# Retention with a gated MLP on one core: the same steps, planned in another order

## The chip, the cores and the metric

One core of one Trainium2 chip runs the whole kernel. The metric is the device time of one execution in microseconds (us), smaller is better. The time before is 221.45 us, the median of three runs (219.28 to 222.36).

## The reference, cut to what matters

A linear attention with a decaying state (retention) feeds a gated MLP. All arrays are float32: 4 batches, 8 heads of 64, 768 tokens, model width 512.

```
for t in range(S):                                  # retention
    state = gamma * state + outer(k[t], v[t])
    y[t] = scale * q[t] @ state
x = y, heads side by side                           # 4 x 768 x 512
gate = sigmoid(sum over 5 taps of conv_w[k] * x shifted by k - 4)
val = x @ w_val                                     # 512 x 512
out = (gate * val) @ w_out                          # 512 x 512
```

## The kernel before, in words

**Tiling.** The 768 tokens are cut into 6 chunks of 128. A chunk of one batch is a *block*: there are 24, numbered g = 0 to 23, chunk by chunk and batch by batch within a chunk, so blocks 0 to 3 are chunk 0 of the four batches. The decay is folded into factors per token: v is scaled on load (`decay`, L294, GpSimd), and y at the end (`evac`, L446, or `wide_evac`, L399, VectorE). So the state is a plain sum, kept in PSUM (`z_ps`).

**Blocks 0 to 3** use whole chunks of 128 tokens ("wide"): `wide_scores` (L347), two masks on VectorE (L355), `wide_y` (L373), `wide_state` (L393) for the running sum, `wide_evac` into the tile x. **Blocks 4 to 23** work on halves of 64 tokens: one `block` on TensorE is 128 small matmuls in four groups, in this order: L403 with the masked scores u, L324 (state, of this block and the next), L403 with `snap` (a copy of the state that ScalarE takes, L334), and L303, the scores of the *next* block. VectorE then masks those (L312) and evacuates y (L446). So block g+1 waits for a mask on VectorE that waits for block g.

**The MLP** works on a chunk of all four batches (512 columns), n = 0 to 5. x and both weights are each split into a high and a low part (fp32r), and a product is three passes: high by high, low by high, high by low. `val_tile` (L592) is 12 matmuls into one bank, `out_tile` (L620) 12 more; there are 4 of each for each n, 288 matmuls of each kind in all. The gate is 5 taps of a convolution: tap 0 on ScalarE (L567), taps 1 to 4 on VectorE (L569), or one or two of them as a matmul with a diagonal on TensorE (`pe_tap`, L578). After that come a sigmoid (L585), the product with val (L601, VectorE), and its split (L608 ScalarE, L612 GpSimd). x is split by L455 (ScalarE) and L459 (GpSimd).

**Weights** arrive as float64 in eight blocks of 512 KB: n = 0 to 3 are the columns of w_val that `val_tile` m = n needs, n = 4 to 7 the rows of w_out. `convert` makes float32 of them in integer steps on VectorE (`cv_bits` L506 or L512, `cv_top` L518, `cv_exp` L524, `cv_rest` L528, `cv_sum` L535, `cv_flush` L542), each on 128x512; then come `cv_round` (L552, ScalarE) and `cv_low` (L556, GpSimd). A block in `FLUSHED` begins on VectorE (L506) and ends with L542; the others begin with three steps on ScalarE (L493, L497, L501) and L512. `cv_sum` is on GpSimd, or on VectorE for the blocks in `SUM_ON_DVE`.

**What sets the order.** Every step is recorded with a due time; `plan` sorts by due time and simulates all engines with costs written in the file, and each engine's instructions are recorded in the order that results. It also picks, for taps 1 and 2, the engine (VectorE or TensorE) that it thinks is free first. On the chip each engine runs its list in order and waits by semaphores. A table of numbers (L655 to L672) sets the due times. All loads of att and the weights go through one queue, SyncE's (SP). A load there also waits until the load issued eight places before it (counted together with ScalarE's four small loads at the start) has landed, and from block 4 on until the buffer of the block four before is free (`LB = 4`).

## Time and profile before

| | us |
|---|---|
| median of three runs | 221.45 |
| lowest, highest | 219.28, 222.36 |
| the profiled execution, its own time | 218.3 |
| its span in the trace | 216.5 |
| TensorE busy | 200.4 |
| VectorE busy | 138.2 |
| ScalarE busy | 109.1 |
| GpSimd busy | 104.4 |

The span is from the first to the last instruction of the profiled execution; the time has 1.8 us more around it. Matmuls overlap in the pipeline, so that one shown with 400 ns in a row of equal ones starts 233 ns after the one before it (12 in 2.80 us). A float32 matmul shows as two records. The engines are named PE (TensorE), DVE (VectorE), ACT (ScalarE), POOL (GpSimd) and SP (SyncE) in the profile.

### The profile page before, as it was taken

The page shows a single profiled execution, that of the slowest core. Times are in us where ns is not written, and L with a number is a line of the kernel's source. Part 1 is how long each engine was busy: PE and PEld are TensorE (multiplying, and loading weights), DVE is VectorE, ACT ScalarE, POOL GpSimd, SP SyncE. Part 2 cuts the span into 40 slices and gives each one's busy share as a digit, 9 for nine tenths or more (in the row PEclk, how much of TensorE's full clock was granted, in tenths as well). Part 3 has the DMA queues.
Part 4 walks back from the last instruction along what each step waited for, and adds up shares of the span by engine and source line. Part 5 has one row for each costly group of instructions (what it writes and reads, how often), then busy time and mean ns, then how long its engine had stood idle before and what let it go on. Part 6 is the DMA issues. An engine that isn't in the chain of part 4 may idle for free.

```text
span 216.5 us, 7441 instructions
## 1 busy us (share of the span) xinstructions
PE 200.4 (93%) x3293; PEld 159.9 (74%) x3293; DVE 138.2 (64%) x213; ACT 109.1 (50%) x224; POOL 104.4 (48%) x93
## 2 busy tenths in 40 slices
PE   8188778989999979999999999999999999999994
PEld 3077666768778758888887888788878887888883
DVE  1959899988999959943993617982189624811000
ACT  2645386397589367456624276341655356321311
POOL 0264599669995954149515078020835145220400
PEclk9769999999999999999999999999999999999999
DMA  6999999886677576076175011101111111111122
GB/s 220 328 414 418 407 381 334 325 300 233 229 272 272 204 248 232 37 233 242 48 221 224 5 48 51 51 9 42 48 51 48 48 48 51 48 48 48 48 97 100
DMA packets 9396, 36.36 MB, mean 168 GB/s; under 512 B 1170, under 2 KB 1682, under 8 KB 6804
## 3 DMA queue, kind: packets, MB, share of 16 engines
q1 hardware_dynamic: 8928, 35.66, 44.7%
q8 instruction: 26, 0.43, 0.8%
q10 hardware_dynamic: 436, 0.23, 0.4%
q14 instruction: 6, 0.05, 0.1%
HBM read 29.59 MB, written 6.29 MB: 166 GB/s over the span
## 4 chain that ended last, share of the span: by engine, by line
PE 76%; DMA 13%; POOL 4%; DVE 3%; ACT 2%; issue 1%; ACTq 0%; SPq 0%; POOLq 0%
PE mm L620 31%; PE mm L592 29%; DMA att<-in_att_dram 11%; PE sy L403 9%; PE z_ps L324 3%; PE sy L303 3%; DMA small_sb<-in_small_dram 2%; POOL xl L459 1%; DVE acc L569 1%; POOL att L294 1%; ACT xh L455 1%; POOL rest L535 1%; DVE gvl L355 1%; POOL wol L556 1%; PE sy L347 1%
## 5 line engine op out<-in xcount | busy, mean ns | idle before, releaser
L569 DVE SCALAR_TENSOR_TENSOR acc<-x,cw_sb,acc 128x512 f32<-128x512 f32 x95 | 68.9, 751 | 22.8 <-ACT acc L567 21.4
L459 POOL TENSOR_TENSOR xl<-x,xh 128x512 fp32r<-128x512 f32 x24 | 30.7, 1296 | 33.6 <-PE mm L592 32.1
L612 POOL TENSOR_TENSOR gvl<-gate,gvh 128x512 fp32r<-128x512 f32 x24 | 30.8, 1295 | 30.6 <-ACT gvh L608 21.0
L620 PE MATMUL mm<-wol,gvh 128*128 128x512 f32 (+1 forms) x100 | 38.9, 389 | 1.1 <-POOL wol L556 1.1
L620 PE MATMUL mm<-woh,gvh 128*128 128x512 f32 (+1 forms) x100 | 39.0, 390 | 0.7 <-ACT woh L552 0.7
L620 PE MATMUL mm<-woh,gvl 128*128 128x512 f32 (+1 forms) x100 | 38.9, 389 | 0.0
L294 POOL TENSOR_TENSOR att<-att,small_sb 128x512 f32<-128x512 f32 x24 | 25.1, 1047 | 24.6 <-DMA att<-in_att_dram 23.6
L630 ACT COPY o_sb<-mm 128x512 f32<-128x512 f32 (+1 forms) x25 | 14.2, 569 | 38.8 <-PE mm L620 37.4
L601 DVE TENSOR_TENSOR gate<-mm,gate 128x512 f32<-128x512 f32 x24 | 16.5, 686 | 26.9 <-PE mm L592 26.6
L592 PE MATMUL mm<-xh,wvh 128*128 128x512 f32 x96 | 27.2, 402 | 1.6 <-ACT xh L455 1.6
L592 PE MATMUL mm<-xl,wvh 128*128 128x512 f32 x96 | 27.6, 400 | 0.0
L592 PE MATMUL mm<-xh,wvl 128*128 128x512 f32 x96 | 27.4, 398 | 0.0
L608 ACT CAST gvh<-gate 128x512 fp32r<-128x512 f32 x24 | 14.9, 620 | 18.0 <-DVE gate L601 12.1
L620 PEld LDWEIGHTS mm<-wol,gvh 128*128 128x128 f32 x100 | 18.8, 188 | 5.5 <-POOL wol L556 1.4
L620 PEld LDWEIGHTS mm<-woh,gvh 128*128 128x128 f32 x100 | 18.8, 188 | 5.0 <-ACT woh L552 0.9
L592 PEld LDWEIGHTS mm<-xh,wvh 128*128 128x128 f32 x96 | 17.6, 188 | 5.8 <-ACT xh L455 1.7
L620 PEld LDWEIGHTS mm<-woh,gvl 128*128 128x128 f32 x100 | 18.8, 188 | 4.1
L592 PEld LDWEIGHTS mm<-xh,wvl 128*128 128x128 f32 x96 | 17.9, 187 | 4.4
L592 PEld LDWEIGHTS mm<-xl,wvh 128*128 128x128 f32 x96 | 17.7, 188 | 4.5 <-POOL xl L459 0.4
L585 ACT ACTIVATE gate<-acc 128x512 f32<-128x512 f32 x24 | 14.3, 597 | 8.9 <-POOL gvl L612 6.1
L334 ACT COPY snap<-z_ps 128x256 f32<-128x256 f32 x40 | 13.4, 374 | 9.4 <-PE z_ps L324 6.6
L403 PEld LDWEIGHTS sy<-u,att 64*64 64x64 f32 x640 | 11.2, 134 | 8.6 <-issue 2.9
(59 smaller groups left out, 263.1 us busy)
## 6 DMA issues: line engine op xcount, KB each, us to landing
att<-in_att_dram SPq DMA_DIRECT2D x20, 1024.0 KB, 6.2
out_dram<-o_sb SPq DMA_DIRECT2D x23, 256.0 KB, 2.0
wst<-in_w_dram SPq DMA_DIRECT2D x8, 512.0 KB, 7.2
att<-in_att_dram SPq DMA_DIRECT2D x3, 768.0 KB, 8.0
att<-in_att_dram SPq DMA_DIRECT2D x5, 256.0 KB, 7.1
att<-in_att_dram SPq DMA_DIRECT2D x1, 512.0 KB, 6.2
out_dram<-o_sb SPq DMA_DIRECT2D x2, 128.0 KB, 1.7
small_sb<-in_small_dram ACTq DMA_DIRECT2D x1, 132.0 KB, 4.3
```

What stands on the lines that cost most here:

```text
L294: nc.gpsimd.tensor_tensor(v, v, vd_sb[:, c, :].unsqueeze(2).broadcast_to([P, 8, HALF]), op=ALU.mult)
L334: nc.scalar.copy(sn, z_ps[:, :, b])
L403: return nc.tensor.matmul(sy[cols, h, off:off + HALF], lhsT=lhsT, rhs=rhs, start=start, stop=True, skip_group_check=True,)
L459: nc.gpsimd.tensor_tensor(xl[n, ct], xs[n][:, ct, :, HALO:], xh[n, ct].bitcast(F32), op=ALU.subtract)
L569: nc.vector.scalar_tensor_tensor(acc, x[:, :, k:k + P], cw_sb[:, m, k:k + 1], acc, op0=ALU.mult, op1=ALU.add,)
L585: nc.scalar.activation(gate[n, m], accs.pop((n, m)), AF.Sigmoid)
L592: nc.tensor.matmul(vps[n, m], lhsT=w[:, m, ct * P:(ct + 1) * P], rhs=xx[n, ct].rearrange("p b t -> p (b t)"), start=(i == 0), stop=(i == 3 ...
L601: nc.vector.tensor_tensor(gv, vps.pop((n, m)), gv, op=ALU.mult)
L608: nc.scalar.copy(gvs[n, m][0], gate[n, m])
L612: nc.gpsimd.tensor_tensor(gvl, gate.pop((n, m)), gvh.bitcast(F32), op=ALU.subtract)
L620: nc.tensor.matmul(ops[n, b, cs.start][:, 0:cs.stop - cs.start], lhsT=gg[:, b * P:(b + 1) * P], rhs=w[:, ct, cs], start=(i == 0), stop=(i ...
L630: nc.scalar.copy(o_sb[:, 0:step], ops.pop((n, b, cs.start))[:, 0:step])
```

## The change

Only the table of numbers changes; every step is still issued once, with the same arithmetic but for three choices: which weight blocks are in `FLUSHED` (five instead of four) and in `SUM_ON_DVE` (two instead of one), and, through the plan, which taps run on TensorE.

```
-    FIRST_LOADS = ((1, 0), (1, 3), (2, 0), (1, 2), (0, 0), (2, 1), (0, 1), (0, 2), (2, 3), (2, 2), (1, 1), (0, 3))
+    FIRST_LOADS = ((1, 0), (0, 0), (1, 1), (1, 2), (2, 1), (0, 1), (1, 3), (2, 0), (0, 2), (0, 3), (2, 2), (2, 3))
...
-    EARLY = 8
+    EARLY = 4
...
-    FLUSHED = (0, 1, 3, 5)
-    SUM_ON_DVE = (3,)
-    BLOCK_AT = (13.32, 26.32, 26.83, 30.27, 39.38, 40.32, 41.28, 42.46, 50.05, 61.09, 68.2, 73.5, 87.54, 92.41, 106.28, 109.98, 121.37, 143.92, 150.84, 184.37)
-    MLP_AT = 39.032
-    MLP_STEP = 4.954
+    FLUSHED = (1, 3, 4, 6, 7)
+    SUM_ON_DVE = (2, 6)
+    BLOCK_AT = (19.76, 27.31, 33.34, 34.76, 39.48, 49.38, 53.2, 56.21, 59.31, 73.82, 79.97, 91.86, 116.18, 119.19, 135.61, 150.42, 153.74, 173.95, 179.78, 208.52)
+    MLP_AT = 28.529
+    MLP_STEP = 8.666
...
-    W_AT = (1.65, 22.94, 24.49, 3.36, 48.39, 41.58, 43.9, 62.46)
+    W_AT = (2.01, 28.62, 23.78, 15.85, 35.37, 56.67, 42.47, 61.42)
```

**SyncE's queue, its first loads before.** 128x1024 of wst is a weight block (512 KB); att_129, att_155, att_178 and att_198 are blocks 0 to 3 and att_279 is block 4; 128x1024 of att is q and k of block 0, 128x1536 is q, k by dimension and v (768 KB), and 128x512 is v of block 0 or the k by token (256 KB). wst_119, wst_124, wst_136 and wst_229 are weight blocks 0, 3, 2 and 1.

```order
L469 DMA wst_119<-in_w64_dram 128x1024
L469 DMA wst_124<-in_w64_dram 128x1024
L282 DMA att_129<-in_att_dram 128x512
L469 DMA wst_136<-in_w64_dram 128x1024
L282 DMA att_129<-in_att_dram 128x1024
L282 DMA att_129<-in_att_dram 128x512
L282 DMA att_155<-in_att_dram 128x512
L282 DMA att_155<-in_att_dram 128x1536
L282 DMA att_178<-in_att_dram 128x1536
L282 DMA att_198<-in_att_dram 128x512
L282 DMA att_178<-in_att_dram 128x512
L469 DMA wst_229<-in_w64_dram 128x1024
```

The thirteenth is q, k and v of block 3. The same queue now, where att_124, att_159, att_207 and att_220 are blocks 0 to 3, and wst_135, wst_140 and wst_178 are weight blocks 1, 2 and 3:

```order
L469 DMA wst_119<-in_w64_dram 128x1024
L282 DMA att_124<-in_att_dram 128x1024
L282 DMA att_124<-in_att_dram 128x512
L469 DMA wst_135<-in_w64_dram 128x1024
L469 DMA wst_140<-in_w64_dram 128x1024
L282 DMA att_159<-in_att_dram 128x512
L282 DMA att_159<-in_att_dram 128x1536
L469 DMA wst_178<-in_w64_dram 128x1024
L282 DMA att_124<-in_att_dram 128x512
L282 DMA att_207<-in_att_dram 128x1536
L282 DMA att_220<-in_att_dram 128x1536
L282 DMA att_207<-in_att_dram 128x512
```

The thirteenth is now the k by token of block 3. The thirteen carry the same bytes. Block 0 has moved from the fifth to the second place, and its k by token from the third to the ninth. Further down, weight block 4 now stands between blocks 6 and 7, where before the next weight blocks stood behind block 7; and on GpSimd's list the sum (L535) of weight block 1 now stands behind the scaling (L294) of block 7, and before stood ahead of that of block 5.

**TensorE, blocks 0 to 3 before,** from the first wide scores to the start of block 4 (L347 scores, L393 state, L373 y):

```order
L347 MATMUL sy<-att 128x128 x8
L393 MATMUL z_ps<-att 64x64 x8
L347 MATMUL sy<-att 128x128 x8
L373 MATMUL mm<-gvl,att 64x128 x8
L393 MATMUL z_ps<-att 64x64 x8
L347 MATMUL sy<-att 128x128 x8
L373 MATMUL mm<-gvl,att 64x128 x8
L393 MATMUL z_ps<-att 64x64 x8
L373 MATMUL mm<-gvl,att 64x128 x8
L347 MATMUL sy<-att 128x128 x8
L393 MATMUL z_ps<-att 64x64 x8
L373 MATMUL mm<-gvl,att 64x128 x8
```

And now, in the same place:

```order
L347 MATMUL sy<-att 128x128 x8
L373 MATMUL mm<-gvl,att 64x128 x8
L347 MATMUL sy<-att 128x128 x8
L393 MATMUL z_ps<-att 64x64 x16
L347 MATMUL sy<-att 128x128 x8
L373 MATMUL mm<-gvl,att 64x128 x8
L393 MATMUL z_ps<-att 64x64 x16
L347 MATMUL sy<-att 128x128 x8
L373 MATMUL mm<-gvl,att 64x128 x16
```

The states of blocks 2 and 3 (the second L393 x16) now stand ahead of the scores of block 3; before, each state stood behind the scores of its block.

**VectorE, from the evacuation of block 3 on, before.** u is the mask of blocks 4 and 5; wst and acc with L518, L524 and L528 are conversions; L569 is the convolution of val tile 0:

```order
L399 TENSOR_TENSOR x<-mm,base 128x4x128
L312 TENSOR_TENSOR u<-sy,small_sb 128x512
L518 SCALAR_TENSOR_TENSOR top<-wst,acc 128x512
L542 SCALAR_TENSOR_TENSOR rest<-acc,rest 128x512
L524 TENSOR_SCALAR acc<-top 128x512
L528 SCALAR_TENSOR_TENSOR rest<-wst,acc 128x512
L569 SCALAR_TENSOR_TENSOR acc<-x,cw_sb,acc 128x512 x3
L446 TENSOR_TENSOR x<-sy,dec 128x4x128
L312 TENSOR_TENSOR u<-sy,small_sb 128x512
```

And now:

```order
L399 TENSOR_TENSOR x<-mm,base 128x4x128
L518 SCALAR_TENSOR_TENSOR top<-wst,acc 128x512
L524 TENSOR_SCALAR acc<-top 128x512
L312 TENSOR_TENSOR u<-sy,small_sb 128x512
L528 SCALAR_TENSOR_TENSOR acc<-wst,acc 128x512
L535 TENSOR_TENSOR rest<-acc,top 128x512
L569 SCALAR_TENSOR_TENSOR acc<-x,cw_sb,acc 128x512
L506 TENSOR_SCALAR acc<-wst 128x512
L569 SCALAR_TENSOR_TENSOR acc<-x,cw_sb,acc 128x512
L518 SCALAR_TENSOR_TENSOR top<-wst,acc 128x512
L569 SCALAR_TENSOR_TENSOR acc<-x,cw_sb,acc 128x512
L446 TENSOR_TENSOR x<-sy,dec 128x4x128
```

Between the evacuation of block 3 and the mask of block 5 there stood nine instructions, and now eleven (the mask of block 5 is the next row); a conversion stands between the taps. From the mask of block 4 to that of block 13, VectorE's list holds the kinds in this table, which counts from just behind the evacuation of block 3 to just ahead of the mask of block 13:

| VectorE | before | now |
|---|---|---|
| steps of conversions | 18 | 28 |
| taps L569 | 19 | 17 |
| masks L312 and evacuations L446 | 18 | 18 |
| products L601 | 4 | 5 |
| in all | 59 | 68 |

How far TensorE's list has come in the MLP when a block begins (matmuls of val, of out, and taps on TensorE issued ahead of it):

| ahead of block | val, out, taps before | val, out, taps now |
|---|---|---|
| 5 | 7, 0, 0 | 8, 0, 1 |
| 8 | 30, 0, 0 | 36, 0, 1 |
| 9 | 36, 0, 0 | 48, 0, 1 |
| 11 | 48, 0, 1 | 59, 0, 2 |
| 13 | 60, 7, 1 | 63, 9, 3 |
| 14 | 67, 9, 1 | 70, 12, 3 |
| 15 | 72, 14, 1 | 72, 24, 3 |
| 19 | 117, 60, 1 | 111, 60, 3 |
| 23 | 204, 152, 1 | 156, 96, 3 |

The list has three taps on TensorE now and had one before; VectorE's taps go from 95 to 93.

14 lines of the change are left out of this document (7 added, 7 removed).

## The prediction

> **What bounds the kernel now.** I read the page first, then the table by windows, the chain of waits, the timelines of TensorE and VectorE, and the DMA issues.
>
> ```profile
> DMA  6999999886677576076175011101111111111122
> ...
> 20.00:80.00 60.00, 52.95 (x1608) 42.06 (x1605) 53.62 (x85) 39.69 (x89) 48.95 (x42) 1.00 0.81 296
> 80.00:200.00 120.00, 119.91 (x1475) 97.16 (x1475) 71.95 (x106) 56.13 (x106) 45.50 (x37) 1.00 0.24 87
> ```
>
> The first row is the busy tenths of the DMA engines in 40 slices of 5.4 us. In the windows the columns are length, then the busy time of PE, PEld, DVE, ACT and POOL, then clock, DMA share and GB/s. From 80 us on TensorE never stops (119.91 of 120 us), so from there the end is a sum of matmuls whose number no order changes. Only what happens before 80 us counts: up to 20 us the DMA engines are full (digits of 9), and from 20 to 80 us VectorE is busy 53.62 of 60 us, as much as TensorE (52.95).
>
> ```profile
> 5.01 6.19 DMA att<-in_att_dram
> ...
> 11.21 10.72 DMA att<-in_att_dram
> ...
> 21.98 1.19 PE sy L347 x16
> ...
> 23.19 1.29 DVE gvl L355 x2
> ```
>
> This is the chain of waits. Block 0 lands at 11.20, block 3 at 21.93; its scores and masks follow. x of chunk 0 is whole when VectorE has evacuated block 3:
>
> ```profile
> 26.18 0.68 DVE L399 TENSOR_TENSOR x<-mm,base 128x512 f32<-128x512 f32 x1
> 26.78 0.68 DVE L312 TENSOR_TENSOR u<-sy,small_sb 128x512 f32<-128x512 f32 x1
> ...
> 68.00 0.68 DVE L312 TENSOR_TENSOR u<-sy,small_sb 128x512 f32<-128x512 f32 x1
> ...
> 26.78:68.00 41.22, 37.58 (x1217) 30.14 (x1218) 38.19 (x61) 30.19 (x69) 37.15 (x32) 1.00 0.80 289
> ```
>
> That is at 26.78, and the second row is the mask of block 4, the third that of block 13. Between them VectorE is busy 38.19 of 41.22 us. Behind the last mask, TensorE goes on:
>
> ```profile
> 69.05 0.69 PE L403 MATMUL sy<-u,att 64*64 64x64 f32 x32
> ...
> 76.21 0.50 PE L620 MATMUL mm<-woh,gvh 128*128 128x512 f32 x1 [0.74 <-ACT woh L552]
> 77.79 0.50 PE L620 MATMUL mm<-wol,gvh 128*128 128x512 f32 x1 [1.08 <-POOL wol L556]
> ...
> 78.36 0.39 PE L592 MATMUL mm<-xh,wvl 128*128 128x512 f32 x1
> ```
>
> Block 13 starts at 69.05. Two last waits, 0.74 and 1.08 us, are for the last weight block. I take 78.36 as the mark: there blocks 4 to 14, 67 matmuls of val, 12 of out and one tap are done, and no wait follows that counts.
>
> **The first stage: block 0 ahead of three weight blocks.** The head of SyncE's queue keeps its sizes (512, 512, 256, 512 KB), so I take its landings over, with other contents.
>
> ```profile
> 0.74 0.85 SPq L469 DMA_DIRECT2D wst<-in_w_dram  x2
> 1.63 0.42 SPq L282 DMA_DIRECT2D att<-in_att_dram  x1
> 2.10 0.43 SPq L469 DMA_DIRECT2D wst<-in_w_dram  x1
> ...
> wst<-in_w_dram SPq DMA_DIRECT2D x1, 512.0 KB, 5.0
> att<-in_att_dram SPq DMA_DIRECT2D x1, 256.0 KB, 6.6
> ...
> wst<-in_w_dram SPq DMA_DIRECT2D x1, 512.0 KB, 7.8
> ```
>
> The second load (issued at about 1.2) lands after 5.0 us, at 6.2; the third at 8.2; the fourth at 9.9. So q and k of block 0 land at about 6.2 instead of 11.20, and its scores start 5 us earlier. I cost this gain at nothing: before x of chunk 0 is whole, block 3 must be in, and the thirteen first loads carry the same bytes as before, over DMA engines that are full. Their last landed at 21.93. Now the last is a piece of 256 KB, and I put it at 21.3, a little earlier, because its predecessor was three times as long. But the order of TensorE puts the state of block 3, which needs that piece, ahead of the scores of block 3.
>
> ```profile
> 14.71 1.16 PE L347 MATMUL sy<-att 64*128 64x128 f32 x16 [0.34 <-DVE gvl L355]
> 15.80 1.09 PE L373 MATMUL mm<-gvl,att 128*64 128x128 f32 x16
> 16.73 0.63 PE L393 MATMUL z_ps<-att 128*64 128x64 f32 x16
> ```
>
> From 21.3: the state 0.63, the scores 1.16, the two masks 1.29, y 1.09, the evacuation 0.68, in all 4.85, give 26.15; with 0.25 for the hand-overs, 26.4. Before it was 26.78. So five microseconds earlier at block 0 become 0.4 at the stage's end. What hides them is the transfer of the rest, with ends at 24.2 (below) and 27.1 (the last piece at 22.0).
>
> **The second stage: VectorE between the evacuation of block 3 and the mask of block 13.** The list holds 59 instructions there before, and 68 now: ten more steps of conversions (the beginnings on VectorE, two sums taken from GpSimd, the later blocks converted sooner), one product more and two taps fewer. Their mean busy time is 38.19 / 61 = 0.626 us, where 61 are the records that the window touches. 68 of them are 42.6 us, if VectorE never waits. With all that VectorE waited before, one instruction is 41.2 / 59 = 0.699 us, and 68 are 47.5. Which end? Before, part of the waiting was of one tap for the next on the same accumulator:
>
> ```profile
> 30.36 2.34 DVE L569 SCALAR_TENSOR_TENSOR acc<-x,cw_sb,acc 128x512 f32<-128x512 f32 x3 [0.39 <-ACT acc L567]
> 33.81 0.74 DVE L569 SCALAR_TENSOR_TENSOR acc<-x,cw_sb,acc 128x512 f32<-128x512 f32 x1
> 34.46 0.68 DVE L506 TENSOR_SCALAR acc<-wst 128x512 int32<-128x512 int32 x1
> ```
>
> Three taps in a row take 2.34 us, 0.78 each; a tap with other work behind it lets that start after 0.65. The new order sets a conversion between the taps. The waits for TensorE and ScalarE stay: behind each mask another mask stands that needs TensorE's block in between, and tap 0 and the sigmoids are queued behind ScalarE's snaps. I take 1.8 us of waiting out of the 3.0 before: 42.6 + 1.8 = 44.4. The mask of block 13 then starts at 26.4 + 44.4 = 70.8 and TensorE's block 13 at about 71.45, 2.4 us later than before.
>
> TensorE has more done by then: 63 + 9 matmuls and three taps against 60 + 7 and one.
>
> ```profile
> 59.38 0.86 PE acc L578 x2
> ...
> 196.58 2.80 PE mm L592 x12
> ```
>
> A matmul is 2.80 / 12 = 0.233 us, a tap on TensorE 0.86 us (one matmul is two records). The two taps more are 1.72 us that the kernel did not have on this engine; they save VectorE 1.3 us, which the count above contains. They are on the path, since TensorE is full afterwards.
>
> **To the mark.** From 71.45: block 13, 2.03 (below); then 7 matmuls of val and 3 of out, 2.33, which makes 75.8; the waits for the last weight block, 0.74 and 1.08 before, should be gone, for its L528 now stands three places ahead of the mask of block 13 on VectorE, and stood five behind it. The mask of block 14 is seven VectorE instructions behind that of block 13: 70.8 + 0.6 + 7 x 0.626 = 75.8, no later. Block 14 ends at 77.85.
>
> ```profile
> 33.94 0.69 PE L403 MATMUL sy<-u,att 64*64 64x64 f32 x32 [0.92 <-DVE u L312]
> 35.97 0.50 PE L592 MATMUL mm<-xh,wvl 128*128 128x512 f32 x1
> ```
>
> These rows are the start of block 5 and the first matmul behind it: a block without a stall is 35.97 - 33.94 = 2.03 us. At 77.85 are done blocks 4 to 14, 70 of val, 12 of out, and all three taps: against the mark three matmuls more, 0.70 us. So TensorE is 78.36 - 77.85 + 0.70 = 1.2 us ahead of before.
>
> **After the mark.** What is left is 9 blocks and the rest of the matmuls on both sides. The blocks come earlier relative to the MLP (block 23 after 252 matmuls instead of 356). The cover for that is VectorE's slack of 48 us in 120 (71.95 busy), and a load of 1 MB per block at 2.6 us (0.4 MB/us) against blocks at least 4 us apart. Were that cover gone, each late mask would cost its wait in full, as the 0.92 us ahead of block 5 did. I take nothing.
>
> **The sum.** The profiled execution took 218.3 us, with a span of 216.5; 218.3 - 1.2 = 217.1. The median of the runs is 3.2 higher than that execution, so for the median 221.45 - 1.2 = 220.2. The three runs lie from 1% below to 0.4% above their median, so what this measurement can tell from no change is about 2%, 4.4 us.
>
> **The rivals.**
>
> *Slower: TensorE's clock falls in the starved first stage.*
>
> ```profile
> 7.60:14.40 6.80, 3.13 (x32) 2.72 (x32) 4.79 (x8) 3.85 (x10) 3.54 (x3) 0.50 1.03 414
> 14.40:22.00 7.60, 6.24 (x114) 5.69 (x114) 6.86 (x15) 4.66 (x15) 3.56 (x4) 1.00 1.02 408
> ...
> 11.24 2.08 PE L347 MATMUL sy<-att 64*128 64x128 f32 x16 [4.78 <-DMA att<-in_att_dram]
> 13.25 1.12 PE L393 MATMUL z_ps<-att 128*64 128x64 f32 x16
> ```
>
> Before, the granted clock was 0.50 from 7.6 to 14.4 us, around TensorE's wait for block 0, and the scores took 2.08 us there instead of 1.16, the state 1.12 instead of 0.63. Now the same work of blocks 0 to 3 is drawn out from 6.5 to 26 us, with gaps from 7.6 to 10 and up to 14, so half clock may last longer. If it is 0.50 up to the evacuation of block 3, state, scores and y of block 3 take 2.9 us longer; if it stays for two further spans of 3.4 us while TensorE waits for VectorE's masks, up to 3.4 more. 220.2 + 6.3 = 226.5. It decides where TensorE is busy less than about 3.13 of 6.80 us from 18 us on; against it stands that half-speed work itself fills that time. [...] Chance 0.09 for the whole, and 0.08 for the 2.9 alone (223.1).
>
> *Faster: the last loads of blocks 2 and 3 land by their latency, not by the bytes ahead of them.*
>
> ```profile
> att<-in_att_dram SPq DMA_DIRECT2D x3, 768.0 KB, 8.0
> att<-in_att_dram SPq DMA_DIRECT2D x5, 256.0 KB, 7.1
> eye_sb<-in_eye_dram ACTq DMA_DIRECT2D x1, 64.0 KB, 8.0
> ...
> 2.12 0.45 ACTq L285 DMA_DIRECT2D eye_sb<-in_eye_dram  x1
> ```
>
> q, k and v of block 3 go out once eye_sb has landed (2.12 + 8.0 = 10.1), so could land at 18.1, and its last piece, issued when the load eight places ahead lands (5.01 + 6.19 = 11.2, a load of the same size in the same place before), at 18.3. Then the masks of block 2 on VectorE are what is late, and x of chunk 0 is whole at 24.2, 2.2 us sooner; with the lower end of VectorE's waits (0.5 us instead of 1.8) the gain is 1.2 + 2.2 + 1.3 = 4.7: 216.7. Against it: 10.72 us for 768 KB in the chain. [...] Chance 0.16.
>
> *No gain: GpSimd stands before a load while a weight waits behind it.*
>
> ```profile
> POOL att L294 <- DMA att<-in_att_dram: 23.6, 12, 6.5
> ```
>
> GpSimd takes its list in order, and waited 23.6 us for loads. Now weight block 1's sum stands behind the scaling of block 7, whose load is behind that of weight block 4 in SyncE's queue. If such a load took 10.72 us instead of the 7 of the other loads, val tile 1 and all that follows start about 3 us later: 223.2. Chance 0.13.
>
> **How the numbers follow.** The forecast has 0.54, and its own range is from 218.5 (VectorE waits 0.5 us, with 0.4 for the scatter of the runs) to 223.3 (all the waits of before, 47.5 us). Faster by over 2% (below 217.0): the faster rival's 0.16 and 0.01 of scatter, 0.17. Slower (over 225.9): the clock's 0.09 and 0.03 for the last two mechanisms together, 0.12. The rest is 0.71. The range from 216.6 to 224.0 leaves out the full clock case, the pairs, and the edge of the faster rival.
>
> **What would show it.** Right: first wide scores at 6.5 to 7 us; the last evacuation L399 between 25.5 and 27.2; the mask of block 13 at 69.5 to 73; TensorE over 99% busy from 80 us on. Wrong: a clock of 0.50 after 20 us; an L399 before 25; waits of TensorE for masks behind 80 us; or GpSimd waits ahead of L535 or L556 that hold up the second val tile.

## The result, and the profile after

The changed kernel took 221.31 us, the median of 21 runs (218.94 to 223.53); the kernel before, beside it, 220.6, the median of 21 (219.1 to 223.29). The ratio is 1.0067, with a 95% interval from 1.0040 to 1.0094: not 1.2 us faster, as forecast, but by this ratio about 0.7% slower. That ratio leaves out runs more than 1.5% above the fastest of their kernel; the runs of these two kernels spread over 2% and more without a gap, so with the experiments the medians of all runs stand too, with 95% intervals from resampling the runs. By those, with all runs of this study together, the changed kernel is at 221.15 (37 runs), before at 220.58 (128 runs): 0.6 us slower (0.2 to 1.1).

The profiled execution of the changed kernel took 218.94 us (span 217.1), that of before 218.3 (216.5). Of the changed kernel, the windows (length; busy PE, PEld, DVE, ACT, POOL; clock; DMA share; GB/s), and then VectorE's and TensorE's timelines:

```profile
20.00:80.00 60.00, 53.71 (x1626) 42.56 (x1627) 56.51 (x90) 36.99 (x82) 48.25 (x42) 1.00 0.79 292
80.00:200.00 120.00, 119.91 (x1475) 96.92 (x1474) 71.49 (x105) 54.96 (x104) 45.40 (x37) 1.00 0.25 90
```

```profile
24.87 0.69 DVE L399 TENSOR_TENSOR x<-mm,base 128x512 f32<-128x512 f32 x1
...
70.03 0.68 DVE L312 TENSOR_TENSOR u<-sy,small_sb 128x512 f32<-128x512 f32 x1
```

```profile
7.46 1.16 PE L347 MATMUL sy<-att 64*128 64x128 f32 x16
...
31.56 0.28 PE L403 MATMUL sy<-att,snap 64*64 64x64 f32 x4 [1.95 <-issue]
...
44.87 0.27 PE L324 MATMUL z_ps<-att 64*64 64x64 f32 x2 [0.37 <-issue]
...
71.06 0.69 PE L403 MATMUL sy<-u,att 64*64 64x64 f32 x32
...
75.61 0.69 PE L403 MATMUL sy<-u,att 64*64 64x64 f32 x32
76.12 0.65 PE L324 MATMUL z_ps<-att 64*64 64x64 f32 x32
76.59 0.65 PE L403 MATMUL sy<-att,snap 64*64 64x64 f32 x32
77.06 0.65 PE L303 MATMUL sy<-att 64*64 64x64 f32 x31
79.35 0.21 PE L303 MATMUL sy<-att 64*64 64x64 f32 x1 [1.65 <-issue]
```

From 80 to 200 us TensorE is as full as before (119.91 of 120). x of chunk 0 is whole at 25.56 (before 26.86), the mask of block 13 is at 70.03, block 13 at 71.06, block 14 at 75.61, and the two waits for the last weight block are gone: all within 0.9 us of the forecast or better. But one matmul record short of the end of block 14, TensorE stands for 1.65 us. The releaser is "issue": the profile shows no semaphore and no data that it waited for. The chain of waits has this stall on it, and the page's table of queues one for instructions:

```profile
29.61 1.95 issue
...
77.70 1.65 issue
```

```profile
q8 instruction: 26, 0.43, 0.8%
```

26 transfers of 16 KB for 3297 matmul records and as many weight loads: about one transfer per 128 matmul records. Before, from 20 us on, TensorE's row has these "issue" stalls:

```profile
30.63 0.28 PE L403 MATMUL sy<-att,snap 64*64 64x64 f32 x3 [0.35 <-issue]
...
44.17 0.62 PE L403 MATMUL sy<-att,snap 64*64 64x64 f32 x26 [0.50 <-issue]
...
48.88 0.27 PE L324 MATMUL z_ps<-att 64*64 64x64 f32 x2 [0.41 <-issue]
```

They are 1.26 us in sum; now there are 1.95, 0.37 and 1.65, in sum 3.97. The waits for data that TensorE's rows show from 26 to 100 us fell by about as much, from 4.3 us to 1.4: in these two profiles the new order did remove waits, and the stalls took the gain back.

### The profile page after: what moved, and what is told of

It is laid out like the page before. It is cut to its first block, busy times and chain, and to the rows that moved or that the text cites. A ratio compares the mean times of both kernels' runs of the same rounds, so it can differ in the third digit from the quotient of the medians.

```text
span 217.1 us, 7461 instructions
## 1 busy us (share of the span) xinstructions
PE 203.7 (94%) x3297; PEld 161.1 (74%) x3297; DVE 138.1 (64%) x213; ACT 107.0 (49%) x222; POOL 103.1 (47%) x92
## 3 DMA queue, kind: packets, MB, share of 16 engines
q1 hardware_dynamic: 8928, 35.66, 44.4%
## 4 chain that ended last, share of the span: by engine, by line
PE 78%; DVE 7%; DMA 5%; issue 3%; ACT 3%; POOL 1%; SPq 0%; ACTq 0%; DVEq 0%; POOLq 0%
PE mm L620 31%; PE mm L592 29%; PE sy L403 8%; DMA att<-in_att_dram 3%; PE sy L303 3%; PE z_ps L324 3%; DMA small_sb<-in_small_dram 2%; PE sy L347 1%; PE z_ps L393 1%; DVE u L312 1%; DVE acc L569 1%; DVE x L446 1%; ACT diag L575 1%; DVE x L399 1%; DVE rest L528 1%
## 5 line engine op out<-in xcount | busy, mean ns | idle before, releaser
L569 DVE SCALAR_TENSOR_TENSOR acc<-x,cw_sb,acc 128x512 f32<-128x512 f32 x93 | 68.0, 752 | 21.3 <-ACT acc L567 20.2
L620 PE MATMUL mm<-woh,gvh 128*128 128x512 f32 (+1 forms) x100 | 39.5, 395 | 0.0
L294 POOL TENSOR_TENSOR att<-att,small_sb 128x512 f32<-128x512 f32 x24 | 25.1, 1047 | 27.1 <-DMA att<-in_att_dram 27.0
L592 PE MATMUL mm<-xh,wvh 128*128 128x512 f32 x96 | 28.4, 410 | 0.8 <-DVE gate L601 0.7
L601 DVE TENSOR_TENSOR gate<-mm,gate 128x512 f32<-128x512 f32 x24 | 16.5, 687 | 19.1 <-PE mm L592 19.1
L592 PE MATMUL mm<-xl,wvh 128*128 128x512 f32 x96 | 26.9, 398 | 0.0
L592 PE MATMUL mm<-xh,wvl 128*128 128x512 f32 x96 | 26.7, 396 | 0.0
L592 PEld LDWEIGHTS mm<-xl,wvh 128*128 128x128 f32 x96 | 17.8, 187 | 6.2 <-issue 1.9
L620 PEld LDWEIGHTS mm<-woh,gvh 128*128 128x128 f32 x100 | 18.8, 188 | 4.7 <-ACT woh L552 0.4
L592 PEld LDWEIGHTS mm<-xh,wvh 128*128 128x128 f32 x96 | 17.6, 188 | 5.9 <-DVE gate L601 1.5
L620 PEld LDWEIGHTS mm<-wol,gvh 128*128 128x128 f32 x100 | 18.8, 188 | 4.1 <-POOL wol L556 0.2
L620 PEld LDWEIGHTS mm<-woh,gvl 128*128 128x128 f32 x100 | 18.8, 188 | 4.1
L592 PEld LDWEIGHTS mm<-xh,wvl 128*128 128x128 f32 x96 | 17.9, 188 | 4.2
L446 DVE TENSOR_TENSOR x<-sy,dec 128x512 f32<-128x512 f32 x20 | 13.7, 686 | 8.6 <-PE sy L303 8.3
```

The lines of the kernel that those rows point to most:

```text
L294: nc.gpsimd.tensor_tensor(v, v, vd_sb[:, c, :].unsqueeze(2).broadcast_to([P, 8, HALF]), op=ALU.mult)
L446: nc.vector.tensor_tensor(xs[c][:, :, b, HALO:].rearrange("p (h j) t -> p h j t", h=2), sy[:, :, 256:512].rearrange("p h (j t) -> p h j t" ...
L569: nc.vector.scalar_tensor_tensor(acc, x[:, :, k:k + P], cw_sb[:, m, k:k + 1], acc, op0=ALU.mult, op1=ALU.add,)
L592: nc.tensor.matmul(vps[n, m], lhsT=w[:, m, ct * P:(ct + 1) * P], rhs=xx[n, ct].rearrange("p b t -> p (b t)"), start=(i == 0), stop=(i == 3 ...
L601: nc.vector.tensor_tensor(gv, vps.pop((n, m)), gv, op=ALU.mult)
L620: nc.tensor.matmul(ops[n, b, cs.start][:, 0:cs.stop - cs.start], lhsT=gg[:, b * P:(b + 1) * P], rhs=w[:, ct, cs], start=(i == 0), stop=(i ...
```

## The experiments

**The theories.** T1, assumed from the count above (26 transfers for 3297 records): TensorE's instructions come in pages of 128 matmul records, the fetch of a page starts when the one before it begins, and where a page is used up faster than the fetch takes, TensorE stalls. By the traces a block is 128 matmul records (64 float32 matmuls, not 128) in 2.03 us, so by T1 a page that falls on a block is used up fastest; the new order changed which work stands where the pages turn. T2: half clock in the starved first stage costs the time, and the stalls are chance. T3: the stall in block 14 is a wait for data that the trace doesn't show.

**Shifting the page turns (three runs).** Tiny matmuls on TensorE shift every later record by their number. In the changed kernel they stand where it waits anyway. The edit, with n = 4 and 20 in the changed kernel and 20 in before:

```
+        def pad(n):
...
+            for _ in range(n):
+                nc.tensor.matmul(
+                    ys[0][:, 0, 0:1], lhsT=warm.broadcast_to([P, P]), rhs=warm,
+                    start=True, stop=True, skip_group_check=True,
+                )
...
         for step in plan(steps):
+            if step.fn is wide_y and step.args == (0,):
+                pad(n)
             step.fn(*step.args)
```

> The changed kernel with 4 tiny bf16 matmuls (128x1) more on TensorE while it waits for the masks of block 0; they write a bank that is overwritten, so no work is left out and nothing after them changes but the count of TensorE's instructions, by 4 matmul records. T1 (a TensorE instruction page of 128 matmul records is fetched as the one before it begins and comes too late where a page is used up faster than the fetch): the page that ended at 77.7 us now ends 4 records sooner in the block, so the stall of 1.65 us inside block 14 shrinks to about 0.8, the one of 1.95 at 29.6 stays near there, and the time falls by 0.5 to 0.9 us against the changed kernel (ratio to before 1.003 instead of 1.007). T2 (the slower clock in the starved first stage costs the time, and the stalls are chance): stalls and time are as in the changed kernel, ratio 1.007. T3 (the stall in block 14 is a wait for data that the trace does not show): the stall stays 1.65 us at the same matmul.

> The same with 20 tiny matmuls (128x1). T1: the page ends move by 20 records, so the stall leaves block 14; the slowest fetch now falls into a block at 60 to 67 us with about 1.0 us of stall, and that at 29.6 us moves 20 records ahead. Time 0.3 to 1.0 us below the changed kernel, ratio to before 1.002 to 1.005. T2: stalls at other places, but the time stays as in the changed kernel, ratio 1.007, with the same spread of the granted clock. T3: 1.65 us of stall stay in block 14 at the same matmul.

> The kernel before with 20 tiny bf16 matmuls (128x1) more on TensorE at the same place (ahead of y of block 0, where it waits). T1: the page ends, which lay well for this order, now lie badly: a new stall of about 1.5 us inside a block at 66 to 69 us, of which the waits of 0.74 and 1.08 us for the last weight block at 75 to 78 us take up part, so the time is 0 to 1.0 us above before, ratio 1.000 to 1.005. T2 and T3: no new stall, ratio 1.000.

Measured: 4 in the changed kernel, median 1.0 us above before (-0.1 to 2.1; ratio 1.0054, 1.0011 to 1.0097); 20 in it, 2.2 above (1.2 to 3.5; 1.0119, 1.0062 to 1.0175); 20 in before, 4.6 above (1.9 to 5.8; 1.0128, 1.0044 to 1.0213). The largest stalls in TensorE's timeline, first with 4, then with 20, then of before with 20:

```profile
80.76 0.34 PE L303 MATMUL sy<-att 64*64 64x64 f32 x5 [1.85 <-issue]
```

```profile
67.17 0.59 PE L578 MATMUL acc<-x,diag 128*128 128x512 f32 x1 [0.67 <-issue]
70.77 0.33 PE L303 MATMUL sy<-att 64*64 64x64 f32 x2 [0.75 <-issue]
76.03 0.45 PE L303 MATMUL sy<-att 64*64 64x64 f32 x11 [0.69 <-issue]
81.67 0.57 PE L303 MATMUL sy<-att 64*64 64x64 f32 x21 [0.91 <-issue]
```

```profile
47.32 0.60 PE L324 MATMUL z_ps<-att 64*64 64x64 f32 x12 [2.23 <-issue]
...
76.97 0.21 PE L303 MATMUL sy<-att 64*64 64x64 f32 x1 [1.73 <-issue]
```

The number of matmul records ahead of each such stall, counted in the trace:

```
before           347  730   858
before, 20 more  347  730  1113  1623
changed          347  729  1750
changed, 4 more  347  729  1750
changed, 20 more 729 1367  1495  1622  1750  1878
```

All lie on 347 plus a multiple of 128, or up to 5 records short of it. The shortfall is TensorE's other instructions: with the weight loads and the semaphore instructions of the trace counted in, the places are 705 (347 + 347 + 11), 1473 (730 + 731 + 12) and 3521 (1750 + 1751 + 20), which is 705 plus 3 and plus 11 times 256. (Another "issue" wait, 0.84 us ahead of record 31 of the changed kernel, is on no such place: it ends 0.10 us after the first mask of block 0 and looks like a wait for that.) With 4 more the stall stayed at record 1750, and so now stands five matmul records from the end of the block instead of one: it goes with the count, not with the instruction. T3 is out. T1's place is right and its sizes are wrong: the stall with 4 more was to shrink to 0.8 and is 1.85, and 20 more made four stalls of 0.7 to 0.9 out of one, with a sum (3.86) that is hardly less. In before, 20 matmuls that compute nothing cost 4.6 us, more than the whole change; its stalls rose from 1.26 to 4.84 us in sum, and two of them have half clock behind them (0.50 from 46.90 to 50.30 and from 77.60 to 81.00). But this price is not of the shift alone, for in before TensorE does not wait at this place:

```profile
16.72 0.69 PE L931 MATMUL mm<-const-float32-0.0 128*128 128x1 bf16 x20
17.34 1.97 PE L373 MATMUL mm<-gvl,att 128*64 128x128 f32 x16
```

The 20 take 0.62 us there themselves, and x of chunk 0 is whole at 28.44, against 26.86 and 27.62 in the two profiles of before.

One reason why the sizes are off shows in the DMA share around block 14, of the changed kernel and then with 4 more:

```profile
75.00:76.00 1.00, 1.00 (x27) 0.59 (x30) 1.00 (x3) 0.59 (x1) 1.00 (x2) 1.00 0.98 418
76.00:77.00 1.00, 1.00 (x83) 1.00 (x76) 0.96 (x3) 0.81 (x2) 0.44 (x1) 1.00 1.01 418
77.00:78.00 1.00, 0.70 (x48) 0.56 (x40) 1.00 (x2) 1.00 (x3) 0.20 (x1) 1.00 0.64 234
```

```profile
77.00:78.00 1.00, 1.00 (x78) 1.00 (x77) 0.96 (x3) 0.61 (x2) 0.67 (x1) 1.00 1.03 426
78.00:79.00 1.00, 0.91 (x59) 0.78 (x52) 1.00 (x2) 1.00 (x3) 0.00 (x0) 1.00 0.84 318
```

In both, the load of a block fills the DMA engines while block 14 runs. The fetch starts at 76.89 in the one and at 78.48 in the other, 1.28 and 1.65 us after the start of block 14, each time as the load ends; it takes 0.9 us, and TensorE goes on 1.35 to 1.55 us after that. The end of the fetch is what ends these stalls: all 61 "issue" stalls over 0.15 us in the 19 traces from 20 to 90 us end 1.2 to 1.6 us after a fetch has landed. What differs is how late the fetch begins and how long the page before lasts by itself (us; runs that stand further down are among them):

```
                     at record  fetch begins  it     page without  stall  from its end
                                after turn    takes  the stall            to TensorE
changed                1750     1.28          0.90   2.24          1.65   1.56
changed, third         1750     1.61          1.00   2.24          1.93   1.42
changed                 347     3.66          1.03   3.98          1.95   1.23
before, 20 more         730     4.08          0.99   4.24          2.23   1.40
changed, 97 more        730     3.91          0.97   3.71          2.64   1.47
```

In block 14 the page is short; at records 347 and 730 it is the fetch that begins late. What makes it begin late is not shown: at record 1750 of the changed kernel the fetch begins as a load ends (DMA share 1.01, then 0.64, above), but at its record 347 the engines are still full when the fetch begins, at 29.30 (1.07 from 29 to 30 us, 1.00 from 30 to 31), so the end of a load is not always what lets it through. Nor does the fetch start when the page before it begins, as T1 had it: in this table it is 1.28 to 4.08 us later.

The places, then, go by 256 of TensorE's instructions, weight loads among them, as counted above. And a turn can cost much in kernels of this case without added matmuls too: up to 2.33 us, at record 347 with five matmuls moved into block 14 (below).

**Second and third profiles, no edit.**

> The changed kernel once more, unaltered, for a second profile. T1, with what the last runs added (the fetch of TensorE's second page is 16 KB on one DMA engine; where it is served while the last loads of the first stage are on that engine, the last of them lands 1.4 us later; and a TensorE stall that leaves a clock window of 3.41 us less than about two thirds busy makes the next window half speed): either the fetch is served at about 19 us and x of chunk 0 is whole at 26.2 to 26.4 us, or at 21 us and it is whole at 24.9 as in the first profile; a stall of 1.6 to 1.9 us at matmul record 1750 in both; a half-clock window behind it in part of the runs. Ratio to before 1.004 to 1.010. Rival (the first profile is typical, and the pads themselves made x of chunk 0 late): 24.9 again.

> The changed kernel unaltered, on the same chip, for the comparison: median of all runs 0.4 to 1.1 us above before. In its profile by T1: a stall of 1.6 us or more at the page turn in block 14, 4 us or more at page turns in sum, x of chunk 0 whole at 25.5 to 25.9 us (or 1.4 later, where the fetch of the second page is served at about 19 us).

> The kernel before once more, unaltered, for a second profile. T1: the same stalls at matmul records 347, 730 and 858, each under 0.8 us and 1.3 us in sum within 0.6; x of chunk 0 whole at 25.4 to 26.8 us, by whether the fetch at about 19.5 us is served ahead of the last load's slowest part; no half clock after 20 us. Rival: stalls at other records or of other sizes, as chance would have them.

Measured: the changed kernel 0.8 us above before (-0.3 to 1.4; ratio 1.0066, 1.0023 to 1.0109) and 0.9 above (-0.5 to 3.0; 1.0151, 1.0101 to 1.0202). Its stall in block 14 came each time, 1.65, 1.94 and 1.93 us; the sum of "issue" stalls was 3.97, 4.45 and 3.61 (4 or more had been expected of the third). Before has 1.26, and now 0.77 and 0.96 = 1.73, but at records 474 and 1879, not at 347, 730 and 858 as expected: the turns are fixed, which of them hurts is not. Its x of chunk 0 was whole at 27.62, later than expected. TensorE of the changed kernel, third profile, its timeline and the windows behind the stall:

```profile
80.89 0.21 PE L303 MATMUL sy<-att 64*64 64x64 f32 x1 [1.93 <-issue]
```

```profile
81.62:85.03 3.41, 3.41 (x10) 2.64 (x9) 3.38 (x6) 1.22 (x2) 1.78 (x2) 0.50 0.32 127
85.03:88.00 2.97, 2.97 (x133) 2.51 (x131) 1.60 (x3) 1.86 (x5) 0.50 (x1) 1.00 0.13 49
```

Behind the stall the clock is 0.50 from 81.62 to 85.03, for 3.41 us, and 1.00 after that. From the start of block 13 to the end of the last matmul it is 142.9 and 143.2 us in the first two profiles, and 144.7 in this one (144.8 with 4 more, where the clock is 0.50 from 81.86 to 85.26): that window costs 1.6 us on top of the stall. Counted in windows of 3.41 us from 16.65, where the half clock of the first profile ended, the same stall was spread over two of them there (0.38 and 1.27 us), and the clock stayed at 1.00. So the profiled execution was a lucky one. In the second profile it is the stall at record 347 that has such a window behind it, from 32.8 to 36.2 us.

The second thing that varies is the last load of the first stage, the 256 KB piece of block 3. Its landing is told in sixteen parts, as many as the profile counts DMA engines; the last two, and when the first 16 KB on the queue for instructions went out:

```
                     15th    16th   fetch, its us
changed             20.44   20.49   21.25  1.06
changed, second     20.48   20.66   21.45  1.10
changed, third      20.51   21.99   19.25  1.12
changed, 4 more     20.53   21.98   19.15  1.12
```

In all traces it goes with that first fetch: where it begins at 19.57 us or sooner (10 traces), the last part lands 1.0 to 1.5 us behind the fifteenth, where it begins at 19.81 or later (9), 0.3 or less. With 97 more it begins at 13.75, and from the load that lands at 16.12 on, every load up to 21.86 has its last part about 1.2 us late: it looks as if one of the engines, which are full (share 1.01 from 9.82 to 16.64 and 1.06 from there to 20 us in the first profile), stays behind by the fetch. x of chunk 0 is whole at 27.07 in the third profile, at 25.56 and 25.74 in the others.

**The clock in the first stage (four runs).** In the changed kernel, eighteen bf16 matmuls of 128x512 and two tiny ones in the waits for block 0 and block 1; in before, four f32 matmuls of zeros in its wait for block 0, or 8 tiny ones with the same page turns. The edit in the changed kernel (`fills` calls `fill`, which stands in it, L378, and is not used there), and that in before:

```
+            if step.fn is wide_y and step.args == (0,):
+                pad(2)
+                fills(0, 10)
+            if step.fn is wide_scores and step.args == (1,):
+                fills(1, 8)
             step.fn(*step.args)
```

```
+        def pad(n):
...
+                nc.tensor.matmul(
+                    ys[0].rearrange("p a t -> p (a t)"), lhsT=zero.broadcast_to([P, P]), rhs=zero.broadcast_to([P, 512]),
...
         for step in plan(steps):
+            if step.fn is wide_scores and step.args == (0,):
+                pad(4)
             step.fn(*step.args)
```

> The changed kernel with 20 bf16 matmuls more on TensorE, as many as in the run with 20 tiny ones (so the page ends lie alike), but 18 of them 128x512: ten at the wait for the masks of block 0 (8.6 to 10.6 us), eight at the wait for block 1 (12.6 to 13.5). They keep TensorE busy where it starved and write banks that are overwritten. T1: the same time as with the 20 tiny ones, within 0.5 us, since x of chunk 0 is late by the loads. T2: the clock stays at 1.00 from 10 to 17 us, its mean rises to about 0.995, the scores and the state there take 1.16 and 0.63 us instead of 2.08 and 1.2, x of chunk 0 is whole 0 to 0.5 us sooner, the spread of the runs shrinks, and the median is 1 us or more below that with the 20 tiny ones.

> The kernel before with four f32 matmuls of zeros (128x512, 8 matmul records) in TensorE's wait for block 0 (7 to 11 us); they write a bank that is overwritten. T2 for before (the half clock after that wait lasts until 14.4 us in the first profile and until 18.8 in the second, and makes x of chunk 0 whole at 26.9 or at 27.6): the clock stays at 1.00 through the first stage, its mean in the runs rises from about 0.969 to 0.985 or more, x of chunk 0 is whole at 26.9 or sooner in every run, and the time is 0.5 to 1.5 us below the same kernel with 8 tiny ones. If the clock in the first stage costs before nothing, as it cost the changed kernel nothing: the same time as with 8 tiny ones, within 0.5 us.

> The kernel before with 8 tiny bf16 matmuls (128x1) at the same place: the page turns of the run with four f32 matmuls, without their hold on the clock. T1: by the durations of before's pages without their stalls this alignment has no page under 3.6 us, as little as now, so ratio 0.997 to 1.003. T2: mean clock 0.961 to 0.977 as in before.

> The kernel before with four f32 matmuls of zeros in TensorE's wait for block 0, once more, beside the changed kernel and before on one chip. T2 for before: median of all runs 0.8 to 1.6 us below that of before, and 1.5 to 2.3 below the changed kernel, mean clock 0.99 to 1.00 in all runs. If the last run was luck of the chip: within 0.5 us of before.

Measured in the changed kernel: 1.5 us above before (0.0 to 2.1; ratio 1.0087, 1.0044 to 1.0131). The clock is full, and the last evacuation starts 0.1 us sooner than with 20 tiny ones (26.23):

```profile
9.82:16.64 6.82, 6.17 (x77) 3.85 (x76) 4.30 (x11) 2.21 (x7) 3.72 (x4) 1.00 1.02 396
```

```profile
26.11 0.69 DVE L399 TENSOR_TENSOR x<-mm,base 128x512 f32<-128x512 f32 x1
```

The median is 0.7 below that with 20 tiny ones (-2.4 to -0.2), between the two expectations, and 6 and 12 runs can't settle that. At a mean clock of 0.99 to 1.00 its runs still spread from 219.7 to 223.4, so T2 is not what spreads them.

In before it is otherwise. The window behind its wait for block 0, in its first profile, its second, and with the four matmuls:

```profile
14.40:18.80 4.40, 4.09 (x72) 3.78 (x74) 3.66 (x10) 1.49 (x6) 3.56 (x4) 1.00 1.03 405
```

```profile
14.40:18.80 4.40, 4.34 (x44) 4.11 (x46) 2.38 (x6) 1.19 (x5) 3.15 (x3) 0.50 1.02 403
```

```profile
14.40:18.80 4.40, 4.40 (x84) 4.09 (x83) 3.40 (x9) 1.24 (x5) 3.15 (x4) 1.00 1.03 405
```

In the second profile the half clock lasts to 18.80 instead of 14.40, TensorE starts 44 matmul records there instead of 72, and x of chunk 0 is whole at 27.62 though the last load landed at 20.56; with the matmuls it is 26.83. Of 107 runs of before, 67 have a mean clock of 0.969 or less, where half clock for 3.41 us is 0.008 (half of 3.41 in a span of 217); its first profile had 0.983. The 67 have a median of 221.05 us, the other 40 of 219.44. With the four matmuls: 1.3 us below before (-2.5 to 0.0; ratio 0.9993, 0.9947 to 1.0039), and again 1.9 below (-3.1 to 0.3; 1.0022, 0.9971 to 1.0073); with 8 tiny ones 0.7 below (-2.4 to 1.4; 0.9993, 0.9941 to 1.0045). The ratios and the medians of all runs agree: the four matmuls don't beat before's good runs, they make the others rare. Their 24 runs have a median of 219.04, against 220.57 of the 39 runs of before beside them (-2.5 to -0.3), and 2.1 us below the changed kernel (1.6 to 3.0). It is the best version found here. The 8 tiny matmuls and the four large ones have the same page turns, but not the same stalls: 3.15 us in sum in the profile of the one, 0.76 and 1.55 in those of the other, and the first of these spans 215.8 us against 218.1. So the sum changes from profile to profile by as much as between the two orders, and with 3.15 us of stalls up to 84 us the time was no longer than that of before. How much of it is the clock and how much the shift by 8 is open: the two differ by 0.6 (-2.3 to 0.9).

**Making the fast pages longer (three runs).** Matmuls of the MLP that stand next to a block on TensorE go into its middle; first five into block 14 alone (run twice), then two to four into each of the blocks 4 to 18:

```
             state(g + 1, 0)
+        for step in inside.get(g, ()):
+            step.fn(*step.args)
         tc.add_manual_dep(
```

> The changed kernel with five matmuls of val (three that stood ahead of block 14 and two that stood behind it) placed in the middle of block 14 on TensorE; nothing is added or left out. T1: the page that held nothing but block 14 now lasts 1.16 us longer, so the stall of 1.65 us at record 1750 shrinks to 0.5 us or less and no half-clock window follows it; the time falls by 1.0 to 2.0 us against the changed kernel, ratio to before 0.998 to 1.003. If the stall is not the cause of the loss (TensorE would catch up later anyway, or the loss lies in the first stage): stall gone or not, the ratio stays 1.006 to 1.008.

> The changed kernel with five matmuls of val in the middle of block 14 once more, since its first profile was taken at a clock of 0.75. T1: the page turn at record 1750 costs 0.7 us or less instead of 1.65 to 1.94, and no other page turn up to 100 us costs over 1 us; where the time is then still that of the changed kernel (221.0), a wait that comes instead must show in TensorE's row.

> The changed kernel with two to four matmuls of the MLP (those that stand next to it on TensorE) in the middle of each of the blocks 4 to 18, nothing added or left out. T1: no page holds more than half a block without a long matmul, so no page lasts under about 2.5 us, and the stalls at page turns up to 100 us fall from 4.5 us in sum to under 2.5, none over 1.2; the changes between small and wide matmuls, 15 more, cost up to 0.3 us each where TensorE is full. Time 0.5 us above to 1.5 us below the changed kernel, ratio 1.000 to 1.009. If the sum of the stalls stays at 4 to 5 us though no page is short (as with block 14 alone), the page's own length is not what sets them, but the fetch.

Measured for block 14 alone: 0.9 above before (-0.2 to 1.8; 1.0182, 1.0122 to 1.0242), where the profiled run went at a clock of 0.75 throughout, took 251 us and tells nothing; again 0.1 above (-0.6 to 1.5; 1.0013, 0.9978 to 1.0048), with this in TensorE's timeline:

```profile
76.89 0.69 PE L403 MATMUL sy<-u,att 64*64 64x64 f32 x32 [0.46 <-DVE u L312]
77.41 0.65 PE L324 MATMUL z_ps<-att 64*64 64x64 f32 x32
77.99 0.50 PE L592 MATMUL mm<-xh,wvl 128*128 128x512 f32 x1
78.33 1.10 PE L592 MATMUL mm<-xl,wvh 128*128 128x512 f32 x4
79.36 0.69 PE L403 MATMUL sy<-att,snap 64*64 64x64 f32 x32
...
81.20 0.33 PE L303 MATMUL sy<-att 64*64 64x64 f32 x3 [0.70 <-issue]
...
87.02 0.46 PE L303 MATMUL sy<-att 64*64 64x64 f32 x15 [0.65 <-issue]
```

The stall in block 14 went from 1.65 to 1.94 down to 0.70, as T1 expected. But the turn at record 347, which was to cost no more than 1 us, took 2.33, so that the stalls are 4.29 us in sum, no less than in the changed kernel. The three matmuls that had stood ahead of the block had covered the wait for its mask (now 0.46), the turn behind block 14 took 0.65, and the change of shapes costs: from L324 to L592 0.58 us instead of 0.47 to the next group of a block, and the five matmuls 1.37 instead of 1.17, together 0.31. Hence little or no gain.

All blocks: 6.1 us above before (5.1 to 7.5; 1.0339, 1.0274 to 1.0405). The only "issue" stalls:

```profile
31.69 0.38 PE L403 MATMUL sy<-att,snap 64*64 64x64 f32 x9 [0.99 <-issue]
...
84.72 0.33 PE L303 MATMUL sy<-att 64*64 64x64 f32 x3 [1.05 <-issue]
```

2.04 in sum instead of 3.6 to 4.5, none over 1.2. The page ahead of the first lasts 4.94 us by itself instead of 3.98, with as late a fetch (3.62 us after the turn), and its stall is 0.99 instead of 1.95: longer pages shorten the stalls, as T1 said. But fifteen splits at 0.31 are 4.7 us, and the waits for data from 26 to 100 us rose to 3.8, from 1.4 to 2.3. The cure costs more than the illness.

**Choosing the turns (two runs).** The same tiny matmuls, 97 in the changed kernel (40 ahead of y of block 0, 57 ahead of the scores of block 1), 107 in before (ahead of the scores of block 0), the numbers that by the pages' durations leave the fewest short pages. In the changed kernel:

```
+            if step.fn is wide_y and step.args == (0,):
+                pad(0, 40)
+            if step.fn is wide_scores and step.args == (1,):
+                pad(1, 57)
             step.fn(*step.args)
```

> The changed kernel with 97 tiny bf16 matmuls (128x1, 0.03 us each) in TensorE's waits for block 0 and block 1 (40 and 57). By the durations of the pages without their stalls, this alignment has the fewest short pages: one of 3.45 us at 34 us and none after it, against one of about 2.2 us at 73 us now. T1 (page turns, longer where a load is on the DMA engines at that time): stalls at page turns 1 to 2 us in sum instead of 4.0 to 4.5, none over 1.2 us, no half-clock window after 20 us, and the time 1.5 to 2.5 us below the changed kernel, ratio to before 0.995 to 1.000. The prediction's gain of 1.2 us would then be there once the page turns are out of the way. If the order itself is slower: stalls down, but the ratio stays over 1.004.

> The kernel before with 107 tiny bf16 matmuls in its wait for block 0, the alignment with the fewest short pages for its order (none under 3.6 us). T1: stalls at page turns 0.5 to 1.2 us in sum instead of 1.3 to 1.7, and the time 0 to 1.0 us below before, ratio 0.995 to 1.000; with 20 tiny ones the same kernel was at 1.013. If any added matmul costs time: ratio above 1.005 again.

Measured: 0.9 above before (-0.1 to 2.1; ratio 1.0008, 0.9976 to 1.0041), and 0.3 below (-3.3 to 2.3; 0.9873, 0.9813 to 0.9933). The second has 1.40 us of stalls in its profile, where 0.5 to 1.2 had been expected. In the first a new stall came at a turn that was to be harmless:

```profile
43.94 0.56 PE L303 MATMUL sy<-att 64*64 64x64 f32 x20 [2.64 <-issue]
```

Its stalls are 4.68 us in sum, where 1 to 2 had been expected. A page's own duration, then, doesn't foretell its stall well enough to choose by: this page lasts 3.71 us, and its fetch began 3.91 us after the turn. Block 14, on the other hand, has no stall here, and the median is still 0.9 above before. The second run shows only that 107 added matmuls cost nothing by the median of 6 runs where TensorE waits for block 0, while 20 cost 4.6 us elsewhere.

**Parts of the change undone (two runs).** The first loads of before with all else as changed (SyncE's first thirteen sorted into the old order; `want` is FIRST_LOADS of before); and the two new taps back on VectorE (with the four tiny matmuls of the first run):

```
+        first.sort(key=lambda s: (want.index(key(s)[:2]), key(s)[2]))
-        for step in order:
+        for step in first + [s for s in order if s not in first]:
             step.fn(*step.args)
```

```
+            if step.fn is pe_tap and step.args[:2] != (0, 3):
+                tap(*step.args)
+            else:
                 step.fn(*step.args)
```

> The changed kernel with the first thirteen loads on SyncE in the order of before; all other steps and the matmul records per page as in the changed kernel. By the prediction (the bytes decide when the last of them lands, 21.3 against 21.9 us): x of chunk 0 whole 0.3 to 1.0 us later than in the changed kernel's second profile (25.7), and the time 0.3 to 1.0 us above it, ratio 1.008 to 1.012. If the new order of the loads gains nothing: ratio 1.006. If the five microseconds at block 0 count in full: x whole at 30 us, ratio 1.025.

> The changed kernel with the two taps that it had moved to TensorE put back on VectorE, at the same places, and four tiny matmuls at the wait of block 0, so that TensorE's pages end at the same records from 67 us on. By the prediction (a tap is 0.86 us of a TensorE that is full afterwards, and 0.65 us of a VectorE that is the limit up to the mask of block 13): TensorE's busy time 1.7 us lower, the mask of block 13 1.3 us later, the time 0 to 0.5 us below the changed kernel, ratio 1.005 to 1.007. If VectorE is not the limit there but TensorE's stalls are: 1.7 us below, ratio 0.999. If VectorE's list costs more than its own time (a tap waiting for the tap ahead of it): 1 us above, ratio 1.011.

Measured: old loads 2.6 us above before (1.6 to 3.7; ratio 1.0107, 1.0067 to 1.0147), so about 2 above the changed kernel. x of chunk 0, with the old loads:

```profile
27.96 0.69 DVE L399 TENSOR_TENSOR x<-mm,base 128x512 f32<-128x512 f32 x1
```

whole at 28.65 instead of 25.6 to 27.1. The last of the thirteen loads landed at 20.53, no later than before. But block 0's scores start at 10.74 instead of 7.46, the clock is 0.50 from 10.54 to 20.79, and TensorE comes to the scores of block 3 only at 24.29 (21.19 in the first profile):

```profile
24.29 1.16 PE L347 MATMUL sy<-att 64*128 64x128 f32 x16 [0.48 <-DVE gvl L355]
```

So with this order on TensorE the early block 0 is worth about 2 us, where the forecast gave it nothing and the loads in all 0.4; with its own order on TensorE, before is whole at 26.86 and 27.62 with the same old loads. Taps back: 2.0 above before (0.3 to 4.3; 1.0114, 1.0052 to 1.0177), of 6 runs. The mask of block 13 is at 71.77, 0.5 later than with 4 tiny matmuls (71.25) instead of 1.3, and TensorE, 1.7 us lighter, waits 4.6 us for data from 26 to 100 us instead of 2.4. So the taps on TensorE gave about what they took; the last of the three expectations (1 us above) is nearest, within what 6 runs tell.

## Why the prediction was wrong, step by step

**The bound.** Right: 119.91 of 120 us on both sides, so what counts is how far TensorE is at 80 us.

**The first stage.** The mechanism was right, the size not: forecast 26.4 for x of chunk 0, measured 25.56, 25.74 and 27.07, against 26.86 and 27.62 before. The last piece landed at 20.49 instead of 21.3. From there to x whole it took 5.1 us in all three profiles, as forecast (4.85 + 0.25), so the path was right. That two of the three came out 0.7 to 0.8 us sooner than forecast is luck: in the third the last part was late. (Two of the prediction's signs missed: the first wide scores start at 7.46 instead of 6.5 to 7, behind other work of TensorE, and the last L399 at 24.87, before 25.) In the trace of before, from which I took the landing, that load had one part 1.1 us late, in the way shown for the changed kernel; that price goes with an early fetch of instructions (at 19.48 us there), and comes and goes in both kernels. Two things the forecast had not: before's own x comes 7.1 us behind its last landing (20.56) in the second profile, where half clock lasts to 18.8, so there TensorE sets it and not the bytes; and the early block 0, costed at nothing, keeps TensorE from being that late in the new order (the run with the old loads).

**The second stage.** Right: 44.4 us forecast from there to the mask of block 13, 44.5 measured (70.03 - 25.56), with VectorE busy 42.66 us of it (42.6 forecast); 44.2 in the third profile, and 46.4 in the second, where the stall of 1.93 us at record 347 and the half clock behind it made VectorE wait longer; the mask at 70.8 forecast, 70.03 measured, block 13 at 71.45 and 71.06, block 14 at 75.8 and 75.61.

**To the mark: the step that failed.** "A block without a stall is 2.03" was used as if a block had none, and block 14 was to end at 77.85. It ended at 79.49 (the rest after the stall starts at 79.35). By the forecast's own sum, 78.36 - 79.49 + 0.70 is -0.4: not 1.2 ahead of before but 0.4 behind, and the last matmul ended at 213.95 instead of 213.40. The missing term is the page turn. It stood in the trace of before as three "issue" stalls of 0.35 to 0.50 us, which I passed over, and in the planner's own constants, estimates written in its file (PAGE, FETCH, CROWDED = 128, 3.4, 6.5). In the new order a page fell on block 14; where TensorE is full, its 1.65 us are lost. Before has as many pages, and by its alignment lost 1.3 to 1.7 us in all. That taking this one stall away would have brought the forecast gain was not shown: with 0.70 us of it left, and in the run with 97 more with none, other turns and waits took its place.

**After the mark.** Right: nothing was taken, and the 0.4 us behind at the mark are 0.55 at the last matmul.

**From the profiled execution to the median.** "The median is 3.2 higher than that execution" was carried over as if it were one offset. It did no harm by luck: with 21 runs the offset is 2.3 in before (220.6 - 218.3) and 2.4 in the changed kernel (221.31 - 218.94). But by the profiles it is different things: in before, most likely half clock in the first stage (its two profiles and the mean clocks of the runs point to it; a mean clock doesn't tell the place); in the changed kernel, a half-clock window behind a stall (1.6 us) and a late last load (1.4 us).

**The rivals.** The slower one had the right resource and the wrong place: the half clock from 9.8 to 16.6 us did not hold up the changed kernel, since its first stage waits for loads; half clock after 20 us did come, by the page turns. Its sum has two further spans of 3.4 us, an estimate; half clock did last 6.83 us in the first profile (9.82 to 16.65), about as long, but no further span followed there. The faster one (last loads by latency, 18.3) fell: no last load landed before 20.4. "GpSimd before a load" fell: TensorE's row shows no wait for the weights of the second val tile. None of the rivals had the cause.

**What stays open.** Why a fetch begins as late as it does (0.6 to 4.3 us after the turn, at the turns with a stall): without that no alignment can be foretold, and the one tried in the changed kernel was foretold wrongly. It is open too how much of the 0.6 us between all runs is stalls, for these vary too much from profile to profile. And the count that would serve the changed kernel best was not found.

## What to carry to other kernels

Read the "issue" rows of an engine that is the bound, however short: where they stand a fixed count of instructions apart (here multiples of 256), they tell where its instruction pages turn, and any change of order, even matmuls that compute nothing, moves other work onto those turns and can cost more than the change itself brings (20 tiny matmuls: 4.6 us of 220, of which 0.6 are their own time). Before a gain of half a per cent is believed, make the same kernel with a few such matmuls more, and take the price from several profiles, not from one. And where TensorE waits long early on and its granted clock falls, a few matmuls in the wait can make the runs alike (before: 219.0 instead of 220.6); in the changed kernel, whose first stage waits for loads, they did not.
